# Up products of the later expert blocks as one 512-column instruction over both parts of x

## The chip, the cores and the metric

One Trainium2 chip, one core of it. The metric is the device time of one execution in microseconds (us). Three executions of the kernel before took 392.26, 396.85 and 391.99 us; their median is 392.26 us.

## What is computed

An RWKV-style linear attention over 4 batches, 8 heads, 768 steps and 48 channels gives 3072 rows of 384 numbers. Each row then goes to one of 8 experts, the one with the highest logit, and the expert's two matrices are applied with a ReLU between them:

```python
logits = x @ w_gate + modality_bias[modality_id]
e_idx = np.argmax(logits, axis=1)
for e in range(E):
    mask = e_idx == e
    h = np.maximum(x[mask] @ w1[e], 0.0)          # 384 -> 1024, "up"
    out[mask] = gate_w[mask, None] * (h @ w2[e])  # 1024 -> 384, "down"
```

All inputs are fp32.

## The kernel before

The first part (to about 150 us) computes the attention, the logits and where each row goes; rows are scattered to a table in DRAM ordered by expert. The second part, which the change touches, runs 12 **blocks** of 256 rows (q = 0 to 11), each of one expert, and then one half block of 128 rows. A program without automatic reordering is emitted (`manual_schedule`): each engine executes its instructions in the order in which the code issues them, and waits in that order.

**Precision by splitting.** A weight matrix w is kept as wh (rounded to the fast fp32 format of the tensor engine) and wl = w - wh; rows and hidden values are split in the same way (xh, xo and hh, hl). A product is the sum of three: high by high, low by high and high by low.

**Weights.** `raw[0]` and `raw[1]` hold the next block's w1 and w2 as loaded. `w_split(k, g)` (line 204) makes group g (a quarter) of them into wh[k] and wl[k]: a cast on ACT (line 206) and a subtraction on VectorE for k = 0 and on GpSimd for k = 1 (line 207). wh and wl exist once, so group g can be split for the next block only when this block's products with group g are done. `blk_raw(q, k)` (line 561) issues two DMAs of 768 KB on SP's queue, which move data only when the expert changes.

**One block**, in the loop of lines 722 to 788:

- The **up phase**: `blk_up(q, g)` for g = 0 to 3 (line 589). Each g has two slices of 128 hidden columns, f = 2g and 2g + 1. A slice takes 9 matmuls of 256 columns (three 128-row pieces c of the 384, three products each), each with its own weight load. The two slices of a g fill one 512-column PSUM bank, by turns pS0, pS1 and pT. ACT then makes hh by a ReLU over the 512 columns (line 601) and VectorE makes hl (line 602). After each `blk_up(q, g)` comes `w_split(0, g)`, for the next block.
- `blk_t` of the next block (line 576): six transposes into the banks pK and pU, an ACT copy to xh and a VectorE subtraction to xo for each bank.
- `blk_raw(nxt2, 0)` (line 757), then `guard_load` (line 759).
- The **down phase**: `blk_down(q, g)` for g = 0 to 3 (line 605), 12 matmuls of 384 columns each, into pY and pX; after each comes `w_split(1, g)`. After g = 1, in blocks 2 to 9, comes `guard` (line 346): two ACT passes over 1152 columns each, which test that the decays are in range.
- In block 9, `flags` (line 526): VectorE sums the guard's result, PE multiplies it by a matrix of ones, VectorE forms the flags. Its matmul stands in PE's order between down(9) and up(10).
- `blk_load` for block q + 2 and `blk_raw(nxt2, 1)` on SP's queue, and `blk_out` (line 616): two scaled ACT copies and two GpSimd DMAs.

The two ends of the change are thus in lines 576 to 603 (what the up products are) and in lines 736 to 787 (where splits and loads stand).

Of the kernel before, what the change touches and what calls it, by code (L numbers as in the profile page):

```python
# [9 lines left out]
F32 = mybir.dt.float32  # L10
F32R = mybir.dt.float32r
BF16 = mybir.dt.bfloat16
I32 = mybir.dt.int32
AF = mybir.ActivationFunctionType
ALU = mybir.AluOpType
# [3 lines left out]
P = 128  # L19
# [5 lines left out]
KC = DM // P  # L25
FC = F // P
XW = DM + 2
NCST = 320 + P + KC * E
BT = 256
# [7 lines left out]
HO = NA + NBX  # L37
# [9 lines left out]
NJ = 2 * NCH  # L47
GW = B * H * S * D // (P * NG)
WHALF = FC // 2 * DM


@with_exitstack
def kernel(ctx: ExitStack, tc: tile.TileContext, rkw, vt, wf, cst, mid, wg, bias, w1, w2, out):
    nc = tc.nc
# [8 lines left out]
    wh, wl = ([cp.tile([P, FC, DM], F32R, name=f"{nm}0")] for nm in ("wh", "wl"))  # L63
# [5 lines left out]
    bp = {"m": ctx.enter_context(tc.tile_pool(name="mp", bufs=1, side="right"))}  # L69
# [11 lines left out]
    def pt(n, tag, sh=(P, 512)):  # L81
        T[tag, n] = ps.tile(list(sh), F32, tag=tag, name=f"{tag}_{n}")
        return T[tag, n]
# [114 lines left out]
    def w_raw(e, k, part, cond=None, parts=2):  # L198
        n = FC // parts
        kw = {} if cond is None else {"cond": cond}  # L200
        nc.sync.dma_start(out=raw[k][:, part * n:part * n + n, :].rearrange("p f c -> p (f c)"),
                          in_=(w1, w2)[k][ds(e, 1), :, part * n * DM:(part + 1) * n * DM].rearrange("a p c -> (a p) c"), **kw)

    def w_split(k, q, n=2, eng=None):
        sl = slice(n * q, n * q + n)
        nc.scalar.copy(out=wh[k][:, sl], in_=raw[k][:, sl])  # L206
        (eng or (nc.vector, nc.gpsimd)[k]).tensor_tensor(out=wl[k][:, sl], in0=raw[k][:, sl], in1=wh[k][:, sl].bitcast(F32), op=ALU.subtract)  # L207
# [34 lines left out]
    def att_iter(i):  # L242
# [29 lines left out]
        if i == NU - 1:  # L272
            blk_t(0)
# [285 lines left out]
    X = {}  # L559

    def blk_raw(q, k):
        if k == 0:
            X["e", q] = (nc.sync.value_load(tab[0:1, 0, q:q + 1], min_val=0, max_val=E - 1),
                         nc.sync.value_load(tab[0:1, 2, q:q + 1], min_val=0, max_val=1))
        e, c = X["e", q]
        for half in range(2):
            w_raw(e, k, half, cond=c != 0)
# [7 lines left out]

    def blk_t(q):
        xl = X["xl", q]
        xh = bp["m"].tile([P, KC, BT], F32R, tag="xh", name=f"xh{q}", bufs=2)
        xo = bp["m"].tile([P, KC, BT], F32R, tag="xo", name=f"xo{q}", bufs=2)
        for c0, c1, tg in ((0, 2, "pK"), (2, 3, "pU")):  # L580
            pp = pt(f"x{q}_{c0}", tag=tg, sh=(P, c1 - c0, BT))
            for c in range(c0, c1):
                for j in range(JT):
                    nc.tensor.transpose(out=pp[:, c - c0, j * P:(j + 1) * P], in_=xl[:, j, c * P:(c + 1) * P], identity=ident)  # L584
            nc.scalar.copy(out=xh[:, c0:c1], in_=pp)
            nc.vector.tensor_tensor(out=xo[:, c0:c1], in0=pp, in1=xh[:, c0:c1].bitcast(F32), op=ALU.subtract)
        X["x", q] = (xh, xo)

    def blk_up(q, g):
        xh, xo = X["x", q]  # L590
        pp = pt(f"u{q}_{g}", ("pS0", "pS1", "pT")[(q * (FC // 2) + g) % 3] if isinstance(q, int) else f"pS{g % 2}", (P, 2, BT))
        for i in range(2):
            f, n = 2 * g + i, 0
            for c in range(KC):
                for wsrc, xsrc in ((wh, xh), (wh, xo), (wl, xh)):
                    nc.tensor.matmul(out=pp[:, i], lhsT=wsrc[0][:, f, c * P:(c + 1) * P], rhs=xsrc[:, c],  # L596
                                     start=(n == 0), stop=(n == 3 * KC - 1))
                    n += 1
        hh = bp["h"].tile([P, 2, BT], F32R, tag="hh", name=f"hh{q}_{g}", bufs=6)
        hl = bp["h"].tile([P, 2, BT], F32R, tag="hl", name=f"hl{q}_{g}", bufs=6)  # L600
        nc.scalar.activation(out=hh, in_=pp, func=AF.Relu)  # L601
        nc.vector.scalar_tensor_tensor(out=hl, in0=pp, scalar=0.0, in1=hh.bitcast(F32), op0=ALU.max, op1=ALU.subtract)  # L602
        X["h", q, g] = (hh, hl)
# [70 lines left out]
    def drain(n):  # L674
        for _ in range(n):
            if pend:
                scatter(pend.pop(0))

    def hook_b(c):
        route_b(c)  # L680
        pend.extend(range(c * NJ, (c + 1) * NJ))
# [40 lines left out]
    for n, q in enumerate(seq):  # L722
        nxt, nxt2 = (seq[n + d] if n + d < len(seq) else None for d in (1, 2))
        if n == len(seq) - 2:
            bad, end, endh, rest = (nc.values_load(flg[0:1, i:i + 1], min_val=lo, max_val=hi)
                                    for i, lo, hi in ((0, 0, P), (1, NQ, HO), (2, HO + NH, NTAB), (3, 0, P + NTAB)))
        if q >= HO:
            for k in range(2):
                half_up(q, k)
            if nxt is not None:  # L730
                half_t(nxt)
            half_down(q)
            blk_out(q, (0,))
            continue

        late = FC // 4 if q == 0 else FC // 2
        for g in range(FC // 2):
            blk_up(q, g)
            if q == 0:
                if g == 0:  # L740
                    x_rows(NU - 1)
                if g < 2:
                    x_cols(NU - 2 + g, pt(("x", g), "pT"))
                else:
                    logits(NU - 4 + g)
                w_split(1, g)
            if (q, g) == (1, 0):
                route_x(1)
            if nxt < HO and g < late:
                w_split(0, g)  # L750
            if q in (2, 3):
                drain(1)
        if q == 0:
            blk_raw(1, 1)
        (blk_t if nxt < HO else half_t)(nxt)
        if q and nxt2 is not None:
            blk_raw(nxt2, 0)
        if 1 <= q <= NG:
            guard_load(q - 1)
        if q == 1:  # L760
            hook_b(1)
        if q == 2:
            tab1 = table(1)
        for g in range(FC // 2):
            blk_down(q, g)
            if q == 0 and g < FC // 2 - late:
                w_split(0, late + g)
            w_split(1, g)
            if q == 0 and g == FC // 2 - late:
                route_a(1)  # L770
            if g == 1 and 2 <= q <= NG + 1:
                guard(q - 2)
            if q == 2:
                drain(1)

            if (q, g) in ((2, 0), (2, 1), (2, 2), (3, 0), (3, 2)):
                next(tab1, None)
            if (q, g) == (2, 0):
                pad_rows()
        if q == 0:  # L780
            blk_raw(2, 0)
        if q == NG + 1:
            flags()
        if nxt2 is not None:
            if nxt2 >= NA:
                fetch(nxt2)
            blk_raw(nxt2, 1)
        blk_out(q)

# [172 lines left out]
```

## Time and profile before

| | |
|---|---|
| Median of three runs | 392.26 us |
| Profiled execution, its own time | 392.17 us |
| Its span, first to last instruction | 390.3 us |
| Outside the span | 1.9 us |
| Mean granted TensorE clock | 0.965 |
| Instructions | 10893 |

The profile's columns: a timeline row has the start in us from the span's start, the duration in us, the engine, the source line, the operation, the tiles as out<-in, the shape and, behind x, the number of instructions merged; a bracket gives the idle time of the engine before it and what ended that. A row of groups has the count, the busy time in us and the mean duration in ns, and then the idle time before. PE is the tensor engine's matmuls, PEld its weight loads, DVE is VectorE, ACT ScalarE, POOL GpSimd, SP the engine whose queue issues the loads. A window row has the width and each engine's busy time in it with the number of instructions begun, then the granted clock, the DMA share and GB/s.

### The profile page before, as it was taken

The numbers are of one execution on the slowest core, as the hardware profiler recorded it, in microseconds if no ns is written. First come the engines' busy times: TensorE is split into PE (matmuls) and PEld (weight loads), VectorE is DVE, ScalarE is ACT, GpSimd is POOL, SyncE is SP. The second block draws the span as 40 slices with busy tenths as digits, with TensorE's granted clock in tenths as the row PEclk, the third lists the DMA queues.
The fourth block names the chain that finished last, engine by engine and source line by source line (L and its number), as shares of the span: only waits on it lengthen the run. The fifth ranks groups of instructions, "written<-read, shape, count | busy, mean of one in ns | idle before, by whom it ended". The sixth has DMA issues, their size and how long they took to land.

```text
span 390.3 us, 10893 instructions
## 1 busy us (share of the span) xinstructions
PE 360.5 (92%) x4280; PEld 343.7 (88%) x4280; DVE 246.7 (63%) x407; ACT 234.1 (60%) x480; POOL 226.3 (58%) x194
## 2 busy tenths in 40 slices
PE   5899899998877999999999999999999999999990
PEld 2688888887866988899999999999999999999990
DVE  6899999999998992675265936344261716651010
ACT  2476466668544662667468586777777675854330
POOL 6234643544878742576688895747466474736440
PEclk9589999999996999999999999999999999999996
DMA  7975779999467851001126543131313474166000
GB/s 153 216 159 135 169 187 215 226 235 211 110 162 193 210 187 51 1 3 42 60 103 223 154 171 117 48 122 39 104 43 101 127 260 135 45 208 196 9 28 21
DMA packets 18464, 50.52 MB, mean 129 GB/s; under 512 B 2917, under 2 KB 10635, under 8 KB 18404
## 3 DMA queue, kind: packets, MB, share of 16 engines
q1 hardware_dynamic: 15268, 40.28, 40.5%
q0 software_dynamic: 3136, 9.47, 6.8%
q8 instruction: 35, 0.57, 0.7%
q14 instruction: 25, 0.20, 0.2%
HBM read 72.89 MB, written 11.63 MB: 217 GB/s over the span
## 4 chain that ended last, share of the span: by engine, by line
PE 64%; DVE 18%; issue 10%; ACT 2%; POOL 2%; DMA 2%; SPq 0%; POOLq 0%; DVEq 0%; ACTq 0%
PE pS_u L596 18%; PE pY_d L613 13%; PE pX_d L613 13%; PE pT_u L596 9%; DVE B L251 5%; DVE A L303 4%; DVE K L221 3%; DVE R L215 3%; PE pS L301 3%; DMA in<-rkw 2%; PE pK_x L584 1%; PE pY L337 1%; PE pK L283 1%; PE pY L331 1%; PE pT L368 1%
## 5 line engine op out<-in xcount | busy, mean ns | idle before, releaser
L207 POOL TENSOR_TENSOR wl<-raw,wh 128x768 fp32r<-128x768 f32 (+1 forms) x60 | 104.1, 1743 | 72.9 <-ACT wh L206 72.8
L206 ACT CAST wh<-raw 128x768 fp32r<-128x768 f32 (+1 forms) x104 | 83.4, 805 | 35.1 <-PE pX_d L613 24.9
L256 POOL TENSOR_TENSOR G<-in 128x512 f32<-128x512 f32 x24 | 31.3, 1303 | 58.4 <-PE pS L301 30.6
L602 DVE SCALAR_TENSOR_TENSOR hl<-pS_u,hh 128x512 fp32r<-128x512 f32 x32 | 22.1, 690 | 55.7 <-ACT hh L601 55.7
L211 ACT COPY pX<-in 128x512 f32<-128x512 f32 x47 | 27.7, 590 | 48.1 <-DVE R L215 39.6
L596 PE MATMUL pS_u<-xh,wh 128*128 128x256 f32 x192 | 54.6, 284 | 0.0
L596 PE MATMUL pS_u<-xo,wh 128*128 128x256 f32 x192 | 54.1, 282 | 0.0
L596 PE MATMUL pS_u<-xh,wl 128*128 128x256 f32 x192 | 54.1, 282 | 0.0
L207 DVE TENSOR_TENSOR wl<-raw,wh 128x768 fp32r<-128x768 f32 x44 | 49.4, 1122 | 2.8 <-ACT wh L206 1.8
L621 POOL DMA_INDIRECT out<-ot,xl x25 | 32.5, 1301 | 10.9 <-ACT ot L620 5.3
L596 PEld LDWEIGHTS pS_u<-xo,wh 128*128 128x128 f32 x192 | 36.2, 189 | 0.0
L596 PEld LDWEIGHTS pS_u<-xh,wl 128*128 128x128 f32 x192 | 36.2, 189 | 0.0
L601 ACT ACTIVATE hh<-pS_u 128x512 fp32r<-128x512 f32 x32 | 19.2, 599 | 28.3 <-PE pS_u L596 28.3
L596 PEld LDWEIGHTS pS_u<-xh,wh 128*128 128x128 f32 x192 | 36.0, 188 | 0.1
L602 DVE SCALAR_TENSOR_TENSOR hl<-pT_u,hh 128x512 fp32r<-128x512 f32 x16 | 11.0, 689 | 39.1 <-ACT hh L601 39.1
L613 PE MATMUL pY_d<-wh,hh 128*128 128x384 f32 x96 | 33.5, 349 | 0.0
L303 DVE TENSOR_TENSOR A<-pS,cs 128x512 f32<-128x512 f32 x48 | 30.7, 681 | 4.0 <-PE pS L301 3.9
L251 DVE TENSOR_TENSOR_SCAN B<-in,d1b 128x516 f32<-128x516 f32 x24 | 30.9, 1288 | 3.5 <-DMA in<-rkw 3.5
L613 PE MATMUL pX_d<-wh,hh 128*128 128x384 f32 x96 | 32.5, 338 | 0.0
L613 PE MATMUL pX_d<-wl,hh 128*128 128x384 f32 x96 | 32.4, 338 | 0.0
L613 PE MATMUL pY_d<-wl,hh 128*128 128x384 f32 x96 | 32.4, 338 | 0.0
L613 PE MATMUL pY_d<-wh,hl 128*128 128x384 f32 x96 | 32.4, 338 | 0.0
(187 smaller groups left out, 910.8 us busy)
## 6 DMA issues: line engine op xcount, KB each, us to landing
raw<-w SPq DMA_DIRECT2D x52, 768.0 KB
in<-rkw SPq DMA_DIRECT2D x46, 288.9 KB
xl<-xs SPq DMA_DIRECT2D x12, 386.0 KB
v<-vt SPq DMA_DIRECT2D x24, 192.0 KB
wg<-wf SPq DMA_DIRECT2D x8, 576.0 KB
raw<-w SPq DMA_DIRECT2D x8, 384.0 KB
xs<-zt SPq DMA_DIRECT2D x8, 193.0 KB
out<-ot,xl POOLq DMA_INDIRECT x25, 3.6
```

The source lines that it names most:

```text
L206: nc.scalar.copy(out=wh[k][:, sl], in_=raw[k][:, sl])
L207: (eng or (nc.vector, nc.gpsimd)[k]).tensor_tensor(out=wl[k][:, sl], in0=raw[k][:, sl], in1=wh[k][:, sl].bitcast(F32), op=ALU.subtract)
L211: nc.scalar.copy(out=pt(a, "pX", (P, 4, P)), in_=src.rearrange("p (a b) -> p a b", a=4))
L215: nc.vector.tensor_tensor(out=R, in0=T["pX", a], in1=T["E", a].rearrange("p (a b) -> p a b", a=4)[:, :, 0:P], op=ALU.mult)
L251: nc.vector.tensor_tensor_scan(out=Bt[:, 516:0:-1], data0=w[:, 516:0:-1], data1=d1b[:, 516:0:-1], initial=0.0, op0=ALU.mult, op1=ALU.max)
L256: ins_g = nc.gpsimd.tensor_tensor(out=G, in0=r, in1=k, op=ALU.mult)
L303: nc.vector.tensor_tensor(out=A[:, hh], in0=pS[hh], in1=mask[:, None, :].to_broadcast([P, 4, P]), op=ALU.mult)
L596: nc.tensor.matmul(out=pp[:, i], lhsT=wsrc[0][:, f, c * P:(c + 1) * P], rhs=xsrc[:, c], start=(n == 0), stop=(n == 3 * KC - 1))
L601: nc.scalar.activation(out=hh, in_=pp, func=AF.Relu)
L602: nc.vector.scalar_tensor_tensor(out=hl, in0=pp, scalar=0.0, in1=hh.bitcast(F32), op0=ALU.max, op1=ALU.subtract)
L613: nc.tensor.matmul(out=X["y", q][j], lhsT=hsrc[:, i, j * P:(j + 1) * P], rhs=wsrc[1][:, f], start=(f == 0 and n == 0), stop=(f == FC - 1 a ...
L621: ins = nc.gpsimd.indirect_dma_start(out=out[:, :], out_offset=bass.IndirectOffsetOnAxis(ap=xl[:, j, DM + 1:DM + 2].bitcast(I32), axis=0), ...
```

## The change

For blocks q >= 3 (`NWIDE = 3`) and below the half block, `up_wide` takes the place of the three-product loop. xh and xo of a block are now the two halves of one tile x2, so that one matmul of 512 columns multiplies wh by both; it fills a whole bank: half 0 gets wh times xh, half 1 wh times xo. A second matmul of 256 columns adds wl times xh to half 0. Each slice has a bank of its own, by turns pS0, pS1, pT, pK and pU. VectorE copies half 1 to SBUF, adds it to half 0 in PSUM, and makes hl one slice later (`rests`); ACT's ReLU works on 256 columns.

In the same blocks `w_split(0, g)` moves from the up phase to the down phase, ahead of `w_split(1, g)`, and `blk_raw(nxt2, 0)` moves from behind `blk_t` to the end of the block, behind the fetch of rows and ahead of `blk_raw(nxt2, 1)`.

```diff
+NWIDE = 3
...
     def blk_t(q):
         xl = X["xl", q]
-        xh = bp["m"].tile([P, KC, BT], F32R, tag="xh", name=f"xh{q}", bufs=2)
-        xo = bp["m"].tile([P, KC, BT], F32R, tag="xo", name=f"xo{q}", bufs=2)
+        x2 = bp["m"].tile([P, KC, 2, BT], F32R, tag="x2", name=f"x2{q}", bufs=2)
+        xh, xo = x2[:, :, 0], x2[:, :, 1]
...
-        X["x", q] = (xh, xo)
+        X["x", q] = x2
+
+    rests = []
+
+    def up_wide(q, g):
+        x2 = X["x", q]
+        hh = bp["h"].tile([P, 2, BT], F32R, tag="hh", name=f"hh{q}_{g}", bufs=6)
+        hl = bp["h"].tile([P, 2, BT], F32R, tag="hl", name=f"hl{q}_{g}", bufs=6)
+        for i in range(2):
+            f = 2 * g + i
+            pp = pt(f"u{q}_{f}", ("pS0", "pS1", "pT", "pK", "pU")[f % 5], (P, 2, BT))
+            for c in range(KC):
+                w = slice(c * P, (c + 1) * P)
+                nc.tensor.matmul(out=pp, lhsT=wh[0][:, f, w], rhs=x2[:, c], start=(c == 0), stop=False, skip_group_check=True)
+                nc.tensor.matmul(out=pp[:, 0], lhsT=wl[0][:, f, w], rhs=x2[:, c, 0], start=False, stop=(c == KC - 1), skip_group_check=True)
+            co = bp["p"].tile([P, BT], F32, tag="co", name=f"co{q}_{f}", bufs=2)
+            nc.vector.tensor_copy(out=co, in_=pp[:, 1])
+            nc.vector.tensor_tensor(out=pp[:, 0], in0=pp[:, 0], in1=co, op=ALU.add)
+            nc.scalar.activation(out=hh[:, i], in_=pp[:, 0], func=AF.Relu)
+            rests.append(lambda hl=hl, hh=hh, pp=pp, i=i: nc.vector.scalar_tensor_tensor(
+                out=hl[:, i], in0=pp[:, 0], scalar=0.0, in1=hh[:, i].bitcast(F32), op0=ALU.max, op1=ALU.subtract))
+            if len(rests) == 2 or f == FC - 1:
+                rests.pop(0)()
+        if g == FC // 2 - 1:
+            rests.pop(0)()
+        X["h", q, g] = (hh, hl)
 
     def blk_up(q, g):
-        xh, xo = X["x", q]
+        if isinstance(q, int) and q >= NWIDE:
+            return up_wide(q, g)
+        x2 = X["x", q]
+        xh, xo = x2[:, :, 0], x2[:, :, 1]
...
-            if nxt < HO and g < late:
+            if nxt < HO and g < late and q < NWIDE:
                 w_split(0, g)
...
-        if q and nxt2 is not None:
+        if 0 < q < NWIDE:
             blk_raw(nxt2, 0)
...
+            if q >= NWIDE and nxt < HO:
+                w_split(0, g)
             w_split(1, g)
...
+            if q >= NWIDE:
+                blk_raw(nxt2, 0)
             blk_raw(nxt2, 1)
```

## The prediction

> **What bounds the kernel now.** I read the page first, then the busy time by stage, then the timeline of PE, ACT, DVE and POOL around one block boundary.
>
> ```profile
> span 390.3 us, 10893 instructions
> PE 360.5 (92%) x4280; PEld 343.7 (88%) x4280; DVE 246.7 (63%) x407; ACT 234.1 (60%) x480; POOL 226.3 (58%) x194
> ```
>
> The windows are the up phase and the down phase of block 7:
>
> ```profile
> 282.00:291.00 9.00, 9.00 (x77) 9.00 (x76) 4.86 (x6) 6.18 (x10) 6.92 (x4) 1.00 0.13 46
> 291.00:300.00 9.00, 9.00 (x56) 9.00 (x54) 2.77 (x5) 6.92 (x11) 3.69 (x2) 1.00 0.36 109
> ```
>
> PE is busy without a hole in both; DVE is idle for 4 of 9 us and for 6 of 9. PE's own starts decide the time of a block:
>
> ```profile
> 281.14 0.34 PE L613 MATMUL pY_d<-wh,hh 128*128 128x384 f32 x1
> ...
> 282.20 0.28 PE L596 MATMUL pS_u<-xh,wh 128*128 128x256 f32 x1
> ...
> 290.84 0.60 PE L584 MATMUL pK_x<-cs,xl 128*128 128x128 f32 x4
> 291.27 0.38 PE L584 MATMUL pU_x<-cs,xl 128*128 128x128 f32 x2
> 291.41 0.42 PE L613 MATMUL pY_d<-wh,hh 128*128 128x384 f32 x1
> ...
> 299.94 0.28 PE L596 MATMUL pT_u<-xh,wh 128*128 128x256 f32 x1
> ```
>
> 72 up matmuls take 290.84 - 282.20 = 8.64 us, 0.120 each; six down matmuls of 384 columns take 282.20 - 281.14 = 1.06, 0.177 each; the block is 299.94 - 282.20 = 17.74 us, its down phase 8.53. A matmul's listed duration (0.28) is not its cost, the distance of starts is.
>
> **The products.** From 256 to 384 columns a start costs 0.057 more, so 512 columns cost about 0.120 + 2 x 0.057 = 0.234 us (no such product is in the trace; bounds: 0.177, as if it cost no more than 384 columns, and 0.240, twice the 256). A pair becomes 0.234 + 0.120 = 0.354 in place of 0.360. A slice is 1.06 us, eight of them 8.50 in place of 8.64: 0.14 us a block, 1.3 us over nine blocks, 14 us at the lower bound (216 x 0.063), if PE still decided. [...]
>
> **DVE's work per slice.** Nearest rows:
>
> ```profile
> L586 DVE TENSOR_TENSOR xo<-pU_x,xh 128x256 fp32r<-128x256 f32 x7 | 2.9, 415 | 0.0
> L602 DVE SCALAR_TENSOR_TENSOR hl<-pS_u,hh 128x512 fp32r<-128x512 f32 x21 | 14.5, 691 | 40.4 <-ACT hh L601 40.4
> L535 DVE COPY fff<-pT_g 128x1 f32<-128x1 f32 x1 | 0.2, 157 | 0.3 <-PE pT_g L533 0.3
> L585 ACT CAST xh<-pU_x 128x256 fp32r<-128x256 f32 x7 | 2.7, 386 | 0.0
> 222.32 0.69 DVE L586 TENSOR_TENSOR xo<-pK_x,xh 128x512 fp32r<-128x512 f32 x1
> 222.92 0.41 DVE L586 TENSOR_TENSOR xo<-pU_x,xh 128x256 fp32r<-128x256 f32 x1
> 205.71 0.17 DVE L456 TENSOR_SCALAR pR_x<-pR_x 128x8 f32<-128x8 f32 x1
> 205.92 0.17 DVE L457 TENSOR_SCALAR pR_x<-pR_x 128x8 f32<-128x8 f32 x1
> ```
>
> The copy from PSUM of 256 columns lies between 0.157 (one column) and the 0.415 of a two-input operation of its size; I take 0.415, the row of its own size and source. [...] The sum into PSUM I take as 0.43, hl as 0.42 (691 less 256 columns at the 1.05 ns between 415 and 684). Independent neighbours start 0.08 before the end (222.32 to 222.92), dependent ones 0.04 after it (205.71 to 205.92). So copy plus sum cost 0.80 (0.415 + 0.04 + 0.35) and hl 0.34: **1.14 us per slice**, over PE's 1.06. The eight need 9.1 us where the whole up phase is 8.50. That alone would be borne, since with five banks DVE may be late by several slices; what counts is when DVE gets to the first copy.
>
> **The moved splits.** ACT's order in the down phase becomes: cast w1 g, cast w2 g for g = 0, 1, then the guard, then g = 2, 3. Behind a down phase now:
>
> ```profile
> 296.71 1.25 ACT L349 ACTIVATE jk<-wg,glo 128x1152 bf16<-128x1152 f32 x1
> 297.87 0.19 ACT L349 ACTIVATION_READ_ACCUMULATOR jk<-wg,glo 128x1 f32 x1
> 298.09 1.26 ACT L350 ACTIVATE jk<-wg,ghi 128x1152 bf16<-128x1152 f32 x1
> 299.25 0.19 ACT L350 ACTIVATION_READ_ACCUMULATOR jk<-wg,ghi 128x1 f32 x1
> 299.35 1.68 ACT L206 CAST wh<-raw 128x768 fp32r<-128x768 f32 x2
> 300.94 0.58 ACT L620 ACTIVATE ot<-pY_d,xl 128x384 f32<-128x384 f32 x1
> ```
>
> The guard takes 2.64 (296.71 to 299.35) and ends 0.6 us before the next up phase (299.94); a cast takes 0.80. Two more casts there put the last w1 cast's end at 299.35 + 1.6 + 0.84 = 301.8, which is 1.85 after the up phase's start. DVE's last w1 subtraction comes behind it, and the first copy behind that. And it meets POOL's:
>
> ```profile
> 227.09 7.28 POOL L207 TENSOR_TENSOR wl<-raw,wh 128x768 fp32r<-128x768 f32 x4
> 232.71 2.49 DVE L207 TENSOR_TENSOR wl<-raw,wh 128x768 fp32r<-128x768 f32 x1
> 235.72 0.94 DVE L207 TENSOR_TENSOR wl<-raw,wh 128x768 fp32r<-128x768 f32 x1
> ```
>
> A DVE subtraction that takes 0.94 alone took 2.49 beside POOL's and ended 0.83 after POOL's last (234.37). So far these stood in different phases. POOL's g = 2 would run from 0.7 to 2.6 after the start, DVE's g = 3 would end 0.83 later, at 3.4 to 3.8 where copies should begin at 1.1.
>
> **The cycle.** Let T be when PE may write bank pU for the next block's last transposes: it waits for hl of slice 4. DVE needs six copies and sums and five hl for that: 6 x 0.80 + 5 x 0.34 + 0.08 = 6.58 us. From T on: DVE's last sum 2.02 (slices 6 and 7), ReLU 0.30, two xh copies 0.77, casts of g = 0 and 1 for w1 and w2 3.2, in all T + 6.3 (PE's g = 1 ends already at T + 4.5); guard 8.9; casts to w1's g = 3 11.3; POOL's g = 2 ends 12.5; DVE's g = 3 ends 13.3; then 6.5: T + 19.8. A block takes **19.8 us in place of 17.74**, +2.1, and PE's product is no part of it. Block 4, where DVE is not late beforehand, gets +1.35; blocks 5 to 9 have +2.1 each, 10.5. Up phases 3 and 11 keep their gain, -0.3.
>
> **The flags.**
>
> ```profile
> 334.94 0.17 DVE L530 TENSOR_REDUCE gsf<-gacc 128x1 f32<-128x16 f32 x1 [5.18 <-ACT jk L350]
> 335.15 0.16 DVE L531 TENSOR_SCALAR gbf<-gsf 128x1 bf16<-128x1 f32 x1
> 335.42 0.18 PE L533 MATMUL pT_g<-gbf,onesb 128*128 128x1 bf16 x1
> 335.46 0.37 PE L596 MATMUL pS_u<-xh,wh 128*128 128x256 f32 x1
> ```
>
> Now the flags' matmul comes as down(9) ends. After the change its input stands on DVE behind w1's g = 3: T + 13.3 + 0.45, where down(9) ends at T + 8.7. PE stands for 5.0 us, up(10) queued behind; DVE's backlog is worked off meanwhile, so 5.0 replaces the 2.1 of a tenth cycle. Even with no DVE lag at all, 1.85 + 0.95 + 0.45 = 3.3 us remain, 4.3 with POOL's hold.
>
> **Sum:** 1.35 + 10.5 + 5.0 - 0.3 = +16.5 us on the profiled execution's 392.17 us (span 390.3 and 1.9 around it; the median is 392.26): **408.7 us**. The bounds of DVE's prices: 0.08 saved at the dependent pair gives 403, 0.03 more on each operation 412; 403 to 412 is this case's own range.
>
> Costed at nothing: the moved load of raw[0]. Its two issues move past guard_load and the fetch on SP's queue and now stand ahead of raw[1]'s; the first half is free by then, the second when DVE's g = 3 is done, 3.8 after the up start, and ACT wants it about 15 us later. Where an expert changes,
>
> ```profile
> 310.00:320.00 10.00, 10.00 (x65) 10.00 (x64) 1.99 (x4) 7.64 (x13) 5.71 (x4) 1.00 0.86 297
> ```
>
> at 297 GB/s four halves take 10.6 us; without that cover 0 to 3 us in each of two blocks. The strided x2 and `co` cost PE nothing: each row of a half is still 256 neighbours.
>
> **Rivals.**
>
> *The copy is cheap* (the other side; time not measurably slower). The point from which it decides: six copies and sums must shrink so that T comes at PE's own 8.9 after the start. At the copy's lower bound 0.157 a slice costs DVE 0.88, and the cycle falls by 8 x 0.26 = 2.1, to PE's 17.6. The stalls vanish; there remain -1.3 and the flags' 4.3: **395.2**. For it: the wide range of that price. Against: the fixed 0.15 of the row of one column plus 1.05 ns a column gives 0.42 again.
>
> *POOL and DVE don't hold each other here* (their subtractions may fall beside one another): DVE's g = 3 is done 1.1 earlier in each cycle. Five cycles of 18.7 give +4.8, block 4 +0.3, the flags 3.6, the two up phases -0.3: **400.6**. For it: many DVE subtractions near POOL work took 0.95. Against: the 2.49.
>
> *The clock gates.* A pause of PE:
>
> ```profile
> 119.87 0.88 PE L331 MATMUL pY<-SPb,R 128*64 128x96 f32 x16 [2.46 <-DVE xp L361]
> 117.00:120.00 3.00, 0.54 (x14) 0.45 (x15) 2.93 (x5) 0.00 (x0) 1.89 (x3) 1.00 0.93 268
> 120.00:128.00 8.00, 8.00 (x108) 7.32 (x109) 6.31 (x10) 4.51 (x12) 7.04 (x8) 0.57 0.68 164
> ```
>
> After 2.46 idle us the granted clock was 0.57 over 8 us, about 6.9 us at half. The flags' 5 us could do the same to up(10): half of 6.9, +3.4: **412.1**. Against: the 2.46 followed sparse work, this pause dense work.
>
> *The wide product is nearly free*: 512 columns at the 0.177 of 384. It pays only if DVE is not the bound; with the cheap copy, 395.2 - 12 = **383**. Against: the 0.057 step from 256 to 384. [...]
>
> **How the numbers follow.** Forecast 0.47, cheap copy 0.25, no hold 0.13, gate 0.13, free product 0.02. What measurement can tell from no change is 2%, 7.8 us, a limit of 400.1. Slower is the forecast, the gate and over half of no hold: 0.68; faster 0.02; same 0.30. The range reaches from the cheap copy, 394, to the gate and the dearest DVE prices, 413.
>
> **What would show it.** Right: 512-column starts 0.23 apart from the next; the first wait of PE in up(5) is before slice 5, released by hl of slice 0 on DVE; DVE's copies in blocks 4 to 9 begin over 3 us after PE's slice 0; blocks of 19 to 20 us; a PE hole of 4 to 5 us before the flags' matmul; blocks 3, 10 and 11 at about 17.6. Wrong: copies under 0.3 us, DVE's w1 g = 3 done within 2 us of the up start, or blocks 4 to 9 below 18 us.

## The result, and the profile after

The changed kernel takes 410.59 us (median of four runs, 410.12 to 415.56) where the kernel before took 392.12 on the same chip: a ratio of 1.0471, 95% interval 1.0358 to 1.0584. It is slower by 18.5 us. Its profiled execution took 410.88 us with a span of 409.1, 18.8 more than before. Its source lines are shifted: casts L207, w subtractions L208, transposes L586, the 512-column product L604, the 256-column one L605, copy L607, sum L608, ReLU L609, hl L611, down products L646.

The page's head, against the one shown of before: DVE's busy time rises from 246.7 to 320.5 us, PE's by 5.4 only.

```profile
span 409.1 us, 10795 instructions
PE 365.9 (89%) x4064; PEld 335.2 (82%) x4064; DVE 320.5 (78%) x587; ACT 238.0 (58%) x516; POOL 229.2 (56%) x194
```

The windows are block 6, from its first up product to the transposes behind the up phase and from there to the next block (the two windows shown of before have PE busy for 9.00 of 9.00 us). PE now has holes, and DVE is busy for 8.2 of 9.5 us.

```profile
271.45:280.96 9.51, 8.76 (x49) 7.27 (x49) 8.20 (x17) 5.63 (x11) 6.64 (x5) 1.00 0.26 62
280.96:290.80 9.84, 9.33 (x57) 9.12 (x56) 7.54 (x14) 7.60 (x15) 4.15 (x2) 1.00 0.21 80
```

PE's rows of the same block, from the timeline. A wide start is followed 0.23 us later by a narrow one, that one 0.12 later by the next wide one. The first wait comes before slice 5 and the second before the last transposes; both are released by DVE's hl.

```profile
271.45 0.39 PE L604 MATMUL pS_u<-x,wh 128*128 128x512 f32 x1
271.68 0.28 PE L605 MATMUL pS_u<-x,wl 128*128 128x256 f32 x1
271.80 0.40 PE L604 MATMUL pS_u<-x,wh 128*128 128x512 f32 x1
...
277.62 0.47 PE L604 MATMUL pS_u<-x,wh 128*128 128x512 f32 x1 [0.75 <-DVE hl L611]
...
282.10 0.41 PE L586 MATMUL pU_x<-cs,xl 128*128 128x128 f32 x2 [0.51 <-DVE hl L611]
```

Why hl is late stands in ACT's and DVE's rows. ACT's last four casts (w1 and w2 of g = 2, 3) start behind the guard, at 271.22. DVE waits for them, its last w1 subtraction takes 2.01 us instead of 0.96 and ends at 275.55, 4.1 us into the up phase. Only then comes the first copy. From there on copies follow each other in 1.12 us.

```profile
271.22 3.02 ACT L207 CAST wh<-raw 128x768 fp32r<-128x768 f32 x4
```

```profile
272.07 0.96 DVE L208 TENSOR_TENSOR wl<-raw,wh 128x768 fp32r<-128x768 f32 x1 [2.06 <-ACT wh L207]
273.54 2.01 DVE L208 TENSOR_TENSOR wl<-raw,wh 128x768 fp32r<-128x768 f32 x1 [0.51 <-ACT wh L207]
275.48 0.41 DVE L607 COPY co<-pS_u 128x256 f32<-128x256 f32 x1
275.93 0.43 DVE L608 TENSOR_TENSOR pS_u<-pS_u,co 128x256 f32<-128x256 f32 x1
...
277.39 0.41 DVE L607 COPY co<-pT_u 128x256 f32<-128x256 f32 x1
277.84 0.43 DVE L608 TENSOR_TENSOR pT_u<-pT_u,co 128x256 f32<-128x256 f32 x1
278.18 0.41 DVE L611 SCALAR_TENSOR_TENSOR hl<-pS_u,hh 128x256 fp32r<-128x256 f32 x1
278.51 0.41 DVE L607 COPY co<-pK_u 128x256 f32<-128x256 f32 x1
```

Two more places lose time. In the timeline around the end of block 3, one DVE subtraction (w1 g = 1) lasts 8.25 us, across all four of POOL's. POOL's row ahead of its four is the last of the scatters of rows, which stand in its queue from 220.92 on. PE waits 3.13 us for DVE's subtraction in the third slice of block 4 and then runs at half clock for 6.8 us (the window row's 0.50).

```profile
225.90 8.25 DVE L208 TENSOR_TENSOR wl<-raw,wh 128x768 fp32r<-128x768 f32 x1
...
225.11 0.97 POOL L556 DMA_INDIRECT xs<-xp,posT  x1 [0.30 <-issue]
226.10 7.22 POOL L208 TENSOR_TENSOR wl<-raw,wh 128x768 fp32r<-128x768 f32 x4
...
234.20 0.58 PE L605 MATMUL pT_u<-x,wl 128*128 128x256 f32 x1 [3.13 <-DVE wl L208]
```

```profile
233.40:240.20 6.80, 6.00 (x19) 5.14 (x20) 6.63 (x20) 1.15 (x3) 2.50 (x2) 0.50 0.40 120
352.90:356.30 3.40, 3.09 (x10) 2.70 (x11) 2.46 (x11) 0.00 (x0) 2.94 (x3) 0.50 0.01 3
```

The second of these windows follows the flags. Their matmul (and its weight load before it) waits 4.5 us for gbf, which stands behind the two late w1 subtractions of block 9 on DVE:

```profile
350.91 1.98 DVE L208 TENSOR_TENSOR wl<-raw,wh 128x768 fp32r<-128x768 f32 x1 [0.51 <-ACT wh L207]
...
353.00 0.16 DVE L532 TENSOR_SCALAR gbf<-gsf 128x1 bf16<-128x1 f32 x1
353.21 0.10 PEld L534 LDWEIGHTS <-onesb 128*128 128x128 bf16 x1 [4.54 <-DVE gbf L532]
```

In the 3.41 us before the first of the two falls (230.00 to 233.41) PE was busy for 1.07 us, before the second (349.47 to 352.88) not at all. Behind PE's pauses of 1.6 us in experiments 1 and 3 below (1.9 on the rows of its weight loads) the products start at full clock's distances: 0.23 and 0.12 us apart in experiment 1, 0.17 to 0.18 in experiment 3's down phase. The last section has more on this.

The lengths of the blocks, from the first up product of one to that of the next, as the two timelines show them:

| block | 3 | 4 | 5 | 6 | 7 | 8 | 9 | 10 | 11 | 3 to 11 |
|---|---|---|---|---|---|---|---|---|---|---|
| before | 17.74 | 17.74 | 17.73 | 17.73 | 17.74 | 17.74 | 17.78 | 17.79 | 17.41 | 159.40 |
| after | 17.48 | 23.64 | 19.24 | 19.35 | 19.33 | 19.35 | 23.78 | 19.00 | 17.18 | 178.35 |

The sum differs by 18.95 us, so the whole loss lies in these blocks. Blocks 3 and 11, whose up phases meet no late DVE, are 0.26 and 0.23 shorter: that is the product itself.

### The profile page after: what moved, and what is told of

It reads as the page before. It is cut to its first block, busy times and chain, and to the rows that moved or that the text cites. A ratio compares the mean times of both kernels' runs of the same rounds, so it can differ in the third digit from the quotient of the medians.

```text
span 409.1 us, 10795 instructions
## 1 busy us (share of the span) xinstructions
PE 365.9 (89%) x4064; PEld 335.2 (82%) x4064; DVE 320.5 (78%) x587; ACT 238.0 (58%) x516; POOL 229.2 (56%) x194
## 4 chain that ended last, share of the span: by engine, by line
PE 33%; DVE 33%; issue 14%; ACT 12%; POOL 3%; DMA 2%; SPq 0%; DVEq 0%; ACTq 0%; POOLq 0%
ACT wh L207 7%; DVE wl L208 6%; PE pY_d L646 5%; DVE B L252 5%; PE pX_d L646 5%; PE pS_u L629 4%; DVE A L304 4%; DVE co L607 3%; DVE K L222 3%; DVE R L216 3%; DVE hl L611 2%; PE pS L302 2%; PE pT_u L629 2%; PE pS_u L604 2%; DVE pS_u L608 2%
## 5 line engine op out<-in xcount | busy, mean ns | idle before, releaser
L208 POOL TENSOR_TENSOR wl<-raw,wh 128x768 fp32r<-128x768 f32 (+1 forms) x60 | 114.7, 1926 | 88.8 <-ACT wh L207 88.7
L207 ACT CAST wh<-raw 128x768 fp32r<-128x768 f32 (+1 forms) x104 | 79.4, 813 | 15.6 <-PE pX_d L646 12.4
L208 DVE TENSOR_TENSOR wl<-raw,wh 128x768 fp32r<-128x768 f32 x44 | 69.5, 1586 | 21.4 <-ACT wh L207 21.2
L604 PE MATMUL pS_u<-x,wh 128*128 128x512 f32 x108 | 41.1, 415 | 3.6 <-DVE hl L611 3.6
L609 ACT ACTIVATE hh<-pS_u 128x256 fp32r<-128x256 f32 x36 | 13.8, 384 | 35.9 <-DVE pS_u L608 32.5
L646 PE MATMUL pY_d<-wh,hh 128*128 128x384 f32 x96 | 33.5, 349 | 0.0
L646 PE MATMUL pX_d<-wh,hh 128*128 128x384 f32 x96 | 32.5, 338 | 0.0
L646 PE MATMUL pX_d<-wl,hh 128*128 128x384 f32 x96 | 32.4, 338 | 0.0
L646 PE MATMUL pX_d<-wh,hl 128*128 128x384 f32 x96 | 32.4, 338 | 0.0
L646 PE MATMUL pY_d<-wl,hh 128*128 128x384 f32 x96 | 32.4, 338 | 0.0
L646 PE MATMUL pY_d<-wh,hl 128*128 128x384 f32 x96 | 32.4, 338 | 0.0
L605 PE MATMUL pS_u<-x,wl 128*128 128x256 f32 x108 | 30.9, 286 | 0.0
L302 PE MATMUL pS<-R,K 64*128 64x128 f32 x384 | 30.7, 304 | 0.0
L302 PEld LDWEIGHTS pS<-R,K 64*128 64x128 f32 x384 | 25.7, 205 | 5.8 <-issue 5.6
L255 DVE TENSOR_TENSOR_SCAN E<-in,d1e 128x516 f32<-128x516 f32 x24 | 29.6, 1233 | 0.8
L556 POOL DMA_INDIRECT xs<-xp,posT x24 | 25.5, 1061 | 7.1 <-issue 5.7
L604 PEld LDWEIGHTS pS_u<-x,wh 128*128 128x128 f32 x108 | 21.1, 196 | 10.0 <-PE pU_u L605 5.0
```

The source lines that it names most:

```text
L255: scan = nc.vector.tensor_tensor_scan(out=Et, data0=w[:, 0:516], data1=d1e, initial=0.0, op0=ALU.mult, op1=ALU.max)
L302: nc.tensor.matmul(out=pS[hh][:, p], lhsT=K[q, p], rhs=R[q, p], start=True, stop=True)
L556: rows_apart("xs", nc.gpsimd.indirect_dma_start(out=xs[:, :], out_offset=bass.IndirectOffsetOnAxis(ap=posT[:, n:n + 1], axis=0), in_=T["xb ...
L604: nc.tensor.matmul(out=pp, lhsT=wh[0][:, f, w], rhs=x2[:, c], start=(c == 0), stop=False, skip_group_check=True)
L605: nc.tensor.matmul(out=pp[:, 0], lhsT=wl[0][:, f, w], rhs=x2[:, c, 0], start=False, stop=(c == KC - 1), skip_group_check=True)
L646: nc.tensor.matmul(out=X["y", q][j], lhsT=hsrc[:, i, j * P:(j + 1) * P], rhs=wsrc[1][:, f], start=(f == 0 and n == 0), stop=(f == FC - 1 a ...
```

## The experiments

Theory A: the product gains 0.25 us a block; the loss comes from DVE reaching the copies late, because w1's splits now end behind the guard on ACT and beside POOL's subtractions, with the flags behind them. Theory B: DVE's 1.12 us per slice, over PE's 1.05, makes the loss wherever the splits stand. Theory C: the half clock is the main cost. Theory D: the hold by POOL has a price of its own. All edits are made to the changed kernel if nothing else is said. "Stretch" is the time from block 3's first up product to the half block's (before 159.40, after 178.35); it leaves out the attention part, which varies by several us from run to run.

### 1. The splits of w1 ahead of the down phase

```diff
+        if q >= NWIDE and nxt < HO:
+            for g in range(FC // 2):
+                w_split(0, g)
         for g in range(FC // 2):
             blk_down(q, g)
...
-            if q >= NWIDE and nxt < HO:
-                w_split(0, g)
             w_split(1, g)
```

> The changed kernel with one thing moved: all four casts and subtractions of w1 stand ahead of the down phase's loop, so ahead of w2's and of the guard on ACT, and ahead of POOL's subtractions. Theory A (DVE comes late to the copies because w1's last subtraction stands behind the guard and POOL): ACT's w1 casts end 0.3 + 0.8 + 4 x 0.73 = 4.0 us after the up phase, DVE is free long before the next one, blocks 3 to 11 take 17.4 to 17.6 us, no pause before the flags' matmul over 0.6 us, no half clock, 390.0 to 391.5 us in all. Theory B (DVE's 1.12 us a slice against PE's 1.06 makes the loss wherever the splits stand): blocks 4 to 9 still over 18.5 us and over 400 us in all.

Measured: 394.94 us, ratio 1.0047 (1.0016 to 1.0077); stretch 162.05. Blocks 3 to 5 take 17.48 to 17.51, as theory A has it, and block 4's hold and both half clocks are gone. But blocks 6 to 8 creep up to 17.72, 17.76 and 17.82, and blocks 9 and 10 take 19.62 and 19.41. So A accounts for the bulk, 16.3 of the 19 us, and B is refuted at its size, but the total is 3.4 us above A's range. ACT's rows at the start of block 8 show what sets the rest. ReLU of slice 7 of block 7 starts at 310.22; then come two xh casts, six casts, the guard, two casts and two output copies, and ReLU of slice 0 can start only at 320.68, 3.6 us into the up phase.

```profile
310.22 0.38 ACT L609 ACTIVATE hh<-pT_u 128x256 fp32r<-128x256 f32 x1 [0.74 <-DVE pT_u L608]
...
318.29 1.55 ACT L207 CAST wh<-raw 128x768 fp32r<-128x768 f32 x2
319.74 0.57 ACT L653 ACTIVATE ot<-pY_d,xl 128x384 f32<-128x384 f32 x1
320.22 0.57 ACT L653 ACTIVATE ot<-pX_d,xl 128x384 f32<-128x384 f32 x1
320.68 0.38 ACT L609 ACTIVATE hh<-pS_u 128x256 fp32r<-128x256 f32 x1
...
328.01 0.38 ACT L609 ACTIVATE hh<-pT_u 128x256 fp32r<-128x256 f32 x1 [0.74 <-DVE pT_u L608]
```

From 310.22 to 320.68 is 10.46 us of ACT in series, from there to slice 7's ReLU at 328.01 are 7.33 us at DVE's pace: a loop of 17.79 us, longer than PE's 17.48. In this form B is true: once ACT is late too, DVE's pace closes a loop that eats the product's gain. The flags' matmul waits 1.94 us for the guard's sum, which ACT now ends later (at 336.17), and then two tiny DVE instructions (L541) last 1.56 and 1.71 us beside POOL's subtractions, which makes up(10) late.

```profile
336.61 0.10 PEld L534 LDWEIGHTS <-onesb 128*128 128x128 bf16 x1 [1.94 <-DVE gbf L532]
...
337.27 1.56 DVE L541 SCALAR_TENSOR_TENSOR fff<-fff 128x1 f32<-128x1 f32 x1
...
338.93 1.71 DVE L541 SCALAR_TENSOR_TENSOR fff<-fff 128x1 f32<-128x1 f32 x1
```

### 2. The guard in the up phase, the splits where the change put them

```diff
+            if g in (0, 2) and NWIDE <= q <= NG + 1:
+                guard(q - 2, (g // 2,))
...
-            if g == 1 and 2 <= q <= NG + 1:
+            if g == 1 and q == 2:
                 guard(q - 2)
```

`guard(n, passes)` now makes one of its two passes per call.

> The changed kernel with the guard's two passes moved into the up phase (blocks 3 to 9); the splits stay where the change put them. Without the guard between them ACT's casts of w2 follow at 1.47 us where a POOL subtraction takes 1.8, so POOL's four would run back to back. Theory A with the hold (a DVE subtraction gets no turn between POOL's back-to-back ones): DVE's w1 g=1 ends only behind POOL's last, about 10 us after the up phase's end, w1 g=3 again about 4 us into the next up phase: blocks 19 us or more, 405 to 412 in all. Theory A without such a hold (the guard's 2.6 us alone make DVE late): w1 g=3 ends about at the up phase's start, blocks 17.6 to 18.0, 393 to 398 in all. Theory B: as the changed kernel, 409 to 412.

Measured: 407.62 us, ratio 1.0365 (1.0302 to 1.0428); blocks 5 to 8 take 18.84 to 19.00, stretch 175.19. So the guard's 2.6 us between the casts are not by themselves what makes DVE late. In the timeline of block 5's end DVE's three last subtractions last 7.08 us beside POOL's four:

```profile
267.88 9.47 POOL L208 TENSOR_TENSOR wl<-raw,wh 128x768 fp32r<-128x768 f32 x4 [6.96 <-ACT wh L207]
268.56 7.08 DVE L208 TENSOR_TENSOR wl<-raw,wh 128x768 fp32r<-128x768 f32 x3 [0.51 <-ACT wh L207]
```

One detail of the expectation was wrong. DVE did get turns: the two engines alternated, 2.03, 2.61 and 2.60 us each for DVE, so w1 g = 3 ended 3.6 us into the up phase, for another reason than a hold across all four.

### 3. The flags one block later

```diff
             blk_down(q, g)
+            if (q, g) == (NG + 2, 0):
+                flags()
...
-        if q == NG + 1:
-            flags()
```

> The changed kernel with the flags' few instructions moved from the end of block 9 to the first step of block 10's down phase. Theory A: the pause of 4.56 us and the half clock behind it go, block 9 takes 19.3 in place of 23.8, block 10 19.0 to 19.4: 406 to 407 in all. Theory C (the half clock is the main cost, and it comes with any lateness of DVE): the gain is smaller than 2 us, since block 10 is still throttled. Theory B: no change outside block 9, the same 406 to 407.

Measured: 410.80 us, ratio 1.0445 (1.0381 to 1.0509), stretch 177.46: A's and B's 406 to 407 was wrong. Block 9 did fall to 19.31, but block 10 rose to 21.24 and block 11 to 18.95. The flags stand behind DVE's backlog wherever they are put (a pause of 1.9 us in down(10)), and the pause in block 9 had been the time in which DVE caught up. Without it the lateness went on: block 10's subtractions, four of DVE beside four of POOL, take 8.53 us and end 4.7 us into up(11). C's size, a gain under 2 us, was met, as there was no gain at all, but not its reason: behind the pause in down(10) the down products start 0.17 to 0.18 us apart (from 364.46 on), as at full clock. Nor can C account for blocks 5 to 8 of the changed kernel, which lost 1.5 to 1.6 us each at full clock (1.00 in block 6's window rows).

```profile
364.16 0.10 PEld L534 LDWEIGHTS <-onesb 128*128 128x128 bf16 x1 [1.90 <-DVE gbf L532]
...
366.83 8.53 DVE L208 TENSOR_TENSOR wl<-raw,wh 128x768 fp32r<-128x768 f32 x4
```

### 4. The kernel before with the moves alone

The edit is made to the kernel before: narrow products, and from block 3 on w1's splits and the load of raw[0] where the change has them.

```diff
-            if nxt < HO and g < late:
+            if nxt < HO and g < late and q < NWIDE:
                 w_split(0, g)
...
+            if q >= NWIDE and nxt < HO:
+                w_split(0, g)
             w_split(1, g)
```

> The kernel before, with its narrow products, and of the change only the moved splits of w1 and the moved load of raw[0] (blocks 3 on). Theory A: DVE is late in every block as in the changed kernel (w1 g=3 ends about 4 us into the up phase), but a narrow up phase asks so little of DVE (0.69 us per pair of slices) that blocks 5 to 8 stay at 17.7 to 17.8; the pause before the flags' matmul is there, 4 to 5 us, with a half clock behind it (up to 1.7 more), and block 4 has its long subtraction and its pause, 3 to 6 us: 400 to 404 in all. Theory B: without the wide product there is no loss: 392 to 393.

Measured: 399.41 us, ratio 1.0156 (1.0094 to 1.0218), stretch 167.76. Blocks 5 to 8 take 17.71 to 17.74 although w1 g = 3 ends 3.8 us into the up phase there too (its row: 267.48 plus 2.01; the up phase starts at 265.74). So lateness alone doesn't lengthen a block. The flags' pause and a half clock of 6.8 us behind it are there, and blocks 9 and 10 take 21.81 and 20.40. Block 4 lost only 1.75, less than expected, and the total is 0.6 us below A's range.

```profile
267.48 2.01 DVE L208 TENSOR_TENSOR wl<-raw,wh 128x768 fp32r<-128x768 f32 x1 [0.51 <-ACT wh L207]
269.64 0.69 DVE L603 SCALAR_TENSOR_TENSOR hl<-pS_u,hh 128x512 fp32r<-128x512 f32 x1 [0.15 <-ACT hh L602]
...
340.71 0.10 PEld L534 LDWEIGHTS <-onesb 128*128 128x128 bf16 x1 [4.18 <-DVE gbf L532]
```

```profile
339.80:346.60 6.80, 5.89 (x28) 5.89 (x29) 3.05 (x11) 0.84 (x2) 4.24 (x3) 0.50 0.27 87
```

### 5. The copy on ACT

```diff
-            nc.vector.tensor_copy(out=co, in_=pp[:, 1])
+            nc.scalar.copy(out=co, in_=pp[:, 1])
...
-            nc.scalar.activation(out=hh[:, i], in_=pp[:, 0], func=AF.Relu)
+            relus.append(lambda hh=hh, pp=pp, i=i: nc.scalar.activation(out=hh[:, i], in_=pp[:, 0], func=AF.Relu))
+            if f:
+                relus.pop(0)()
...
-            if len(rests) == 2 or f == FC - 1:
+            if len(rests) == 3:
                 rests.pop(0)()
```

The ReLU and hl thus both come one slice later than in the changed kernel.

> The changed kernel with the copy of the second half of the bank made by ACT in place of DVE; ACT's ReLU goes one slice later for it, the splits stay where the change put them. DVE's work per slice falls from 1.12 to about 0.77 us, ACT's rises from 0.38 to about 0.75. This is the rival of the prediction with a cheap copy: lateness at the start of the up phase (about 4 us) remains, but DVE and ACT work off a slice in 0.77 where PE makes one in 1.05. Theory A: the last transposes wait little or not, blocks 5 to 8 take 17.5 to 18.0 us; the pause before the flags' matmul (about 4.5 us) and block 4's (about 5) remain: 399 to 403 in all. If lateness alone costs, whatever the work per slice: blocks 5 to 8 stay over 19 us and 409 to 412 in all.

Measured: 404.89 us, ratio 1.0304 (1.0251 to 1.0357), stretch 171.31: 1.9 us over A's range. Blocks 5 to 8 take 18.15 to 18.20 in place of 19.35. w1 g = 3 still ends 3.7 us into the up phase (275.50, against a start of 271.76), and the late slices are then worked off at 0.67 us each (276.57 to 277.24 to 277.90), where the changed kernel takes 1.12. PE's wait before slice 5 shrinks from 0.75 to 0.27. So it takes both: lateness at the start, and a pace at which DVE can't make it up before PE needs a bank again. Block 4 (22.28), the flags' block (22.25) and block 10 (19.27) kept most of their losses; A's range had left out block 10's.

```profile
276.57 0.43 DVE L608 TENSOR_TENSOR pT_u<-pT_u,co 128x256 f32<-128x256 f32 x1 [0.38 <-ACT co L607]
...
277.24 0.42 DVE L608 TENSOR_TENSOR pK_u<-pK_u,co 128x256 f32<-128x256 f32 x1
...
277.47 0.47 PE L604 MATMUL pS_u<-x,wh 128*128 128x512 f32 x1 [0.27 <-ACT hh L609]
...
277.90 0.42 DVE L608 TENSOR_TENSOR pU_u<-pU_u,co 128x256 f32<-128x256 f32 x1
```

### 6. The wide product alone

```diff
-            if nxt < HO and g < late and q < NWIDE:
+            if nxt < HO and g < late:
                 w_split(0, g)
...
-            if q >= NWIDE and nxt < HO:
-                w_split(0, g)
             w_split(1, g)
```

The load of raw[0] goes back to its place too.

> The changed kernel with the move undone: w1's splits stand again between the slices of the up phase and raw[0]'s load where it was; only the wide product with its copy and sum is left of the change. Theory A: each subtraction of w1 (0.95 us) stands on DVE in order between two pairs of slices and waits for ACT's cast, which waits for the ReLU before it, so DVE needs about 2 x 1.12 + 1 to 2 per pair: up phases of 11 to 13 us, blocks of 20 to 21.5 us, no pause for the flags; 412 to 425 in all. If the product itself decided, as its arithmetic says (0.14 us less per block), it would be 390 to 391.

Measured: 427.16 us, ratio 1.0891 (1.0858 to 1.0925), stretch 194.37; blocks 3 to 10 take 20.6 to 23.4. The direction is A's, the size a little over its range. In the timeline of up(4), after the ReLU of slice 1 ACT casts w1 g = 0 (0.83 us), DVE waits 0.91 us for it and subtracts (0.96), and only then copies slice 2, which stood ready. A pair of slices takes 4.12 us of DVE (238.79 to 242.91), and PE makes one in 2.1. The move was therefore no mere extra: without it the wide product costs 35 us.

```profile
238.79 0.96 DVE L208 TENSOR_TENSOR wl<-raw,wh 128x768 fp32r<-128x768 f32 x1 [0.91 <-ACT wh L207]
239.67 0.42 DVE L607 COPY co<-pT_u 128x256 f32<-128x256 f32 x1
...
242.91 0.96 DVE L208 TENSOR_TENSOR wl<-raw,wh 128x768 fp32r<-128x768 f32 x1 [0.91 <-ACT wh L207]
```

### 7 and 8. POOL's subtraction behind DVE's

Both runs keep the changed kernel's casts and guard, and only order POOL's subtractions: the first lets each of w2 g wait for DVE's of w1 g + 1, the second only g = 2 (and in block 3 g = 0 too). The edit shown is the second's; `w_cast` makes the cast alone and `w_sub` POOL's subtraction, which waits for the instruction `sub` where one is given.

```diff
             if q >= NWIDE and nxt < HO:
-                w_split(0, g)
-            w_split(1, g)
+                sub = w_split(0, g)
+                if g == 3 or (q, g) == (NWIDE, 1):
+                    w_sub(1, g - 1, sub)
+                w_cast(1, g)
+                if g in (1, 3) or (q > NWIDE and g == 0):
+                    w_sub(1, g)
+            else:
+                w_split(1, g)
```

> The changed kernel with one added order: POOL's subtraction of w2 g starts only when DVE's of w1 g+1 is done, so that the two never run side by side; all else, the guard and the casts on ACT too, stands as in the changed kernel. Theory D (the hold by POOL has its own price): w1 g=3 ends 1.05 us earlier, about 3.0 us into the up phase; block 4 loses its long subtraction and its half clock (23.6 to about 18.5), blocks 5 to 8 take 18.2 to 18.4 us in place of 19.34, the flags' pause is 3.5: 399 to 402 in all. If the hold only shifts work that would be late anyway: blocks 5 to 8 at 19.2 to 19.4 and over 405 in all.

Measured: 409.38 us, ratio 1.0406 (1.0367 to 1.0445), stretch 176.20. Block 4 fell to 19.21, but blocks 5 to 8 rose to 19.56: POOL's g = 1, now behind the guard, held DVE's g = 3 instead. So the total missed D's range.

```profile
249.55 1.85 POOL L217 TENSOR_TENSOR wl<-raw,wh 128x768 fp32r<-128x768 f32 x1 [2.23 <-DVE wl L208]
...
249.98 2.23 DVE L208 TENSOR_TENSOR wl<-raw,wh 128x768 fp32r<-128x768 f32 x1 [0.51 <-ACT wh L207]
```

> The order of the run before it, mended: there POOL's g=1, delayed behind DVE's g=2 and so behind the guard, held DVE's g=3 for 2.23 us itself, so the hold was only passed on. Now POOL's g=1 runs at once, during the guard, and only POOL's g=2 waits for DVE's g=3 (in block 3 POOL's g=0 waits for DVE's g=1 too). The rest is the changed kernel. Theory D (the hold has its own price of 1.05 us per cycle): w1 g=3 takes 0.95 and ends about 3.0 us into the up phase, blocks 5 to 8 take 18.2 to 18.4 us in place of 19.34, the flags' pause is 3.5 in place of 4.56, block 4 about 18.5 to 19.2 in place of 23.6: 399 to 402 in all. If the hold only shifts work that would be late anyway: blocks 5 to 8 at 19.2 to 19.4, 404 or more in all.

Measured: 409.61 us, ratio 1.0366 (1.0267 to 1.0465), stretch 171.41. DVE's g = 3 takes 0.96 and ends 3.1 us into the up phase (278.14, start 275.07), and blocks 5 to 8 take 18.18 to 18.32: theory D holds, the hold is worth 1.05 us in each cycle, as much as it delays DVE. The flags' block fell to 21.70. The total missed D's range: the stretch is 6.9 us shorter, but this execution began block 3 5.5 us later than the changed kernel's, in the attention part, and block 4 took 22.72 although no DVE subtraction there was held. In its block 3 two of ACT's casts of w2 waited, the second until the down phase's end, so that DVE came to w1 g = 3 only at 240.00, 5.8 us into block 4: the block was late by ACT this time. The load of this w2 was issued 4.0 us before ACT was free for the first of the two casts (224.73 and 228.76), in the changed kernel 5.5 us (217.35 and 222.85). A late load would fit the first wait, but the record has no time of its landing; the cause stays open.

```profile
277.18 0.96 DVE L208 TENSOR_TENSOR wl<-raw,wh 128x768 fp32r<-128x768 f32 x1 [0.51 <-ACT wh L207]
278.06 0.42 DVE L617 COPY co<-pS_u 128x256 f32<-128x256 f32 x1
```

### 9. Splits, guard and flags moved

Experiments 1 and 2 together, and `flags()` called in block 9's down phase behind g = 2 (`if (q, g) == (NG + 1, 2)`).

> The changed kernel with three things moved: w1's casts and subtractions ahead of the down phase's loop, as in the first experiment; the guard's two passes into the up phase (blocks 3 to 9); the flags' instructions into block 9's down phase before its last quarter. In the first experiment ACT reached the first ReLU 3.6 us into the up phase (ReLU of slice 7, two xh casts, six casts, guard 2.6, two casts, two output copies: 10.4 us), and DVE's seven slices of 1.12 us closed a cycle of 17.76 us. Without the guard that cycle is 15.1 us, below PE's own 17.48. Theory A with that cycle: all blocks from 3 on take 17.45 to 17.55 us, no pause for the flags over 0.3, 389.5 to 390.5 in all (0.4 to 0.7% below the kernel before). Theory B (the work per slice itself is too much): blocks 6 to 8 still 17.7 to 17.8, 392 or more in all.

Measured: 391.11 us, ratio 0.9968 (0.9949 to 0.9986), stretch 158.23. Blocks 3 to 8 take 17.48 to 17.51: with ACT's guard out of the loop the product's gain is there in each of them, and B is refuted. The total is 0.6 us above A's range. Blocks 9 and 10 took 18.05 and 18.01: the flags' matmul waited 0.58 us behind w1's four subtractions, and the two instructions of L541 were held again (0.73 and 1.72 us).

### 10 to 12. The flags taken apart, and the wide product from block 1

The sum and comparison of the flags go ahead of w1's splits in block 9, the matmul and one copy stay behind g = 2, the rest goes to the end of up(10).

> The kernel with splits, guard and flags moved, and its flags taken apart: the sum and comparison ahead of w1's splits of block 9, the matmul and its copy where they were, the rest at the end of block 10's up phase, when POOL's subtractions are over. There blocks 9 and 10 took 18.05 and 18.01 us: 0.57 of pause before the flags' matmul (behind w1's four subtractions on DVE) and 0.5 of lateness from two tiny two-input instructions on DVE that took 0.73 and 1.72 us beside POOL's subtractions. Theory A: both blocks take 17.5 us, 1.0 us less in all, 389.8 to 390.5. Theory B: unchanged, 391.

Measured: 395.70 us beside 396.40 for the kernel before, ratio 0.9999 (0.9950 to 1.0048); stretch 157.30, with block 9 at 17.62 and block 10 at 17.50. The blocks did what A said; the total couldn't tell, as the runs of before beside it spread over 7 us. It was timed once more:

> The kernel with splits, guard and flags moved and the flags taken apart, timed once more, since the runs of the kernel before beside the first timing spread from 391.7 to 398.8 us and left an interval of half a per cent to each side. By its blocks (17.5 us from block 3 on, 17.6 for block 9, 157.3 us from block 3's first up product to the half block's, where the kernel before takes 159.4) it should be 2.1 us faster: a ratio of 0.993 to 0.996. If the blocks' gain is given back elsewhere in the program, the ratio is 0.999 to 1.001.

Measured: 390.22 us beside 392.00, ratio 0.9968 (0.9940 to 0.9995); stretch 157.29. This is the fastest version by its blocks, 2.1 us under before. By the whole time it is 0.3%, a little less than the 0.4 to 0.7% expected, and the interval only just excludes no difference. PE is again busy without a hole over a whole block, with 0.24 us less of it. The window is one block of this run, and its timeline shows the starts 17.50 apart:

```profile
264.90:282.40 17.50, 17.50 (x104) 16.42 (x103) 13.55 (x30) 13.11 (x25) 9.65 (x7) 1.00 0.25 79
```

```profile
264.21 0.39 PE L609 MATMUL pS_u<-x,wh 128*128 128x512 f32 x1
...
281.71 0.39 PE L609 MATMUL pS_u<-x,wh 128*128 128x512 f32 x1
```

The same with `NWIDE = 1`:

> The same kernel with the wide product from block 1 on in place of block 3, the splits and the guard moved there too. If DVE has room in blocks 1 and 2 as in the later ones, each gains 0.25 us: 0.5 us less in all than with block 3. Against it: the routing's instructions stand on DVE in blocks 1 and 2 (blocks of 18.31 and 17.73 us now); if they meet the copies, DVE is late there and the blocks grow to 18.5 us or more, with the lateness carried on: 1 to 4 us more in all.

Measured: 396.86 us, ratio 1.0046 (1.0003 to 1.0088). Blocks 1 and 2 gain 0.23 each (18.08 and 17.50 in place of 18.31 and 17.73), but blocks 3 and 4 take 18.44 and 18.04: 1.0 us more in all by the blocks, at the lower end of the second forecast. The routing's instructions do meet the copies, but a block later than forecast: in the timeline of block 2's end they stand on DVE behind the four splits, from 213.26 to 218.5, so that block 3's first copy comes at 218.49, 3.1 us after its first product, and PE waits 0.51 us before the last transposes.

## Why the prediction was right, and where it wasn't

The time, 410.59, lies 1.9 us above the forecast of 408.7 and inside its range, 1.5 below the rival with the gated clock; the mechanism of the regular blocks was the one forecast; that the sum came so near is partly luck (see below). By its own steps:

- **The product.** 0.234 a start was forecast, 0.23 measured (271.45 to 271.68), and blocks 3 and 11 gained 0.26 and 0.23 where 0.14 was said. The narrow products out of the strided x2 start 0.12 before the next (271.68 to 271.80), where those out of a tile of their own took 0.120.
- **DVE's prices.** Copy 0.415, sum 0.43 and hl 0.42 were forecast, 0.41, 0.43 and 0.41 measured; a slice costs 1.12 in place of 1.14. The rival with a cheap copy is out.
- **The moved splits.** w1 g = 3 was to end 3.4 to 3.8 us after the up phase's start; it ended 4.1 after it. The hold of 1.05 us is there, and experiment 8 shows that it counts in full.
- **The cycle.** 19.8 was forecast, 19.24 to 19.35 measured: 0.5 too much, most of it because casts in a row follow each other in 0.73 us (four take 3.02 in all), not in 0.80, and the cycle has seven of them. Lateness and pace were the two halves of the argument, and the experiments show them apart: late with the narrow products' little work on DVE, a regular block loses nothing (4); late with a pace of 0.67, it takes 18.15 (5); on time with a pace of 1.12, it takes 17.5 (9).
- **The flags.** 5.0 forecast, 4.5 measured. That this pause also let DVE catch up was in the text; that removing it would gain nothing (experiment 3) was not foreseen.
- **Block 4.** This is the term that was mis-sized: +1.35 was forecast and +5.90 measured. The 1.35 is given without its working, and the step "Block 4, where DVE is not late beforehand" overlooked block 3's scatters on POOL, although the prediction shows POOL's four subtractions of that block back to back (227.09). POOL came to its four subtractions only at 226.10, and then, back to back, they held DVE's w1 g = 1 for 8.25 us. That the hold made most of the loss is borne out by the first run of experiments 7 and 8, where POOL waits for DVE and block 4 takes 19.21.
- **The half clock.** It was a rival with 0.13 and came twice, 6.8 and 3.4 us long; the prediction had only the second place in mind. At half clock these cost at most 3.4 and 1.7 us of PE, half of each by estimate. For block 4 PE's starts tell the wait and the clock apart: the narrow product due 0.23 behind the start at 230.69 came at 234.20, 3.3 us late, and from there to 240.30 nine pairs and a narrow product took 6.10 us, where starts of 0.35 and 0.12 give 3.28, 2.8 us more. Together these are the 6.2 us over a block of 17.48. So the wait, not the clock, made the larger part of block 4's loss.

The sum came out near because two errors offset each other. Block 4 was 4.55 too low; the cycles with the flags were 2.0 too high (10.5 + 5.0 forecast, 12.3 measured in blocks 5 to 9 and 1.2 in block 10); the up phases' gain was 0.2 too small. Blocks 10 and 11 were named at about 17.6; block 10 took 19.00, and this was the half clock: PE has no wait in it behind the flags' matmul, and the half clock covers its first 3.0 us: its first six pairs take 3.60 us (353.26 to 356.86), where starts of 0.35 give 2.1, which costs 1.5.

## What to carry to other kernels

Here an engine whose work per stage is a little over the bound's (1.12 us a slice beside 1.05) was harmless where it started on time (blocks of 17.5 us in experiment 9), and a fixed lateness of 3.8 us was harmless where it could be made up (17.71 to 17.74 in experiment 4); the two together were paid in every round (19.24 to 19.35), so cost both. When work is moved, follow the whole in-order queue that it moves into, on each engine: here it was the guard on ACT, POOL's subtractions and the flags behind them, and not the product, that decided, and moving those gave the product's gain back in the blocks (17.5 us in place of 17.74). A pause that is removed can give nothing if another engine used it to catch up (410.80 us in experiment 3 beside 410.59).

## What the runs showed of the hardware

DVE's subtractions of w1 and POOL's of w2 held each other in three ways. In experiment 2 they took turns, about 2.6 us for each (a DVE subtraction alone takes 0.96, a POOL one 1.84). In the changed kernel's blocks 4 to 9 two of a block's four DVE subtractions lasted 2.0, and two of POOL's in a row 4.4, where two in a row take 3.65 in the kernel before (247.03). At the end of block 3 POOL's four ran back to back in 7.22 us, and DVE's, recorded as started 0.2 us before them, ended 0.83 behind the last. What decides which engine is held was not shown. The size of the DVE operands is no measure of the hold: in experiment 3 an instruction on 128x1 elements (L541) lasted 1.64 us beside a subtraction of POOL (364.60 to 366.44), and 0.16 behind it, at 366.56.

Beside plain fp32 the rounded format took less per column in the kernel before: the half block's up products, plain fp32 with 128 columns, start 0.11 us apart (five of them in 0.72 us from 375.46 on, the last of them 0.27 long), those of the rounded format with 256 columns 0.120.

A half clock shows in the products' starts as well: in the changed kernel a wide product was followed by a narrow one after 0.43 us and that one by the next after 0.21, 1.9 and 1.8 times the 0.23 and 0.12 at full clock.

In the traces of the two kernels the granted clock changed only at whole steps of 3.41 us from its first change. At full clock, a step with at most 1.18 us of PE's work was followed by a half clock: in the changed kernel 1.07 and 0.00 us in the blocks, and in both kernels one with about 1 us before the blocks (in the kernel before 0.95 from 117.32 to 120.73, with the pause of 2.46 us in it) and one at the start, with 1.18 and 1.16. The steps with 1.96 us or more were not. Whether PE's work in a step or its longest wait tells the two apart was not shown.
